# Attention and MLP kernel on one Trainium2 core: the last chunk of batch 0 in a new order, and v of block 2 transposed on TensorE

## The chip, the cores and the metric

The kernel runs on one core of a Trainium2 chip. The metric is the device time of one execution in microseconds; the time before is 698.05 us, the median of 4 runs (697.73 to 698.29). Inside one core the engines run beside each other, each working off its own queue in order: TensorE (PE) multiplies, VectorE (DVE) and ScalarE (ACT) work element by element, GpSimd (POOL) and SyncE (SP) here mainly issue DMAs. An instruction waits at the head of its queue until the semaphores it needs are set.

## What is computed

```python
# q, k, v: (4, 6080, 256) float32; w_in: (256, 2048); w_out: (2048, 256)
qn = q / (np.linalg.norm(q, axis=1, keepdims=True) + 1e-06)
kn = k / (np.linalg.norm(k, axis=1, keepdims=True) + 1e-06)
s = kn.transpose(0, 2, 1) @ qn / tau          # (4, 256, 256)
a = softmax(s, axis=-1)
x = (v @ a).reshape(4 * 6080, 256)
h = x @ w_in
out = gelu_tanh(h) @ w_out                    # (24320, 256)
```

The norms run over the 6080 tokens, so all of a batch's q and k must have been read before its 256x256 attention matrix exists. The kernel folds that matrix into the first weight: h = v @ (a @ w_in), with `aw` = a @ w_in, so that per token only two large products are left.

## The kernel before

**Statistics of a batch.** q^T k (the Gram matrix G) and the sums of squares are collected over chunks of rows. For batch 0 this stands ahead of everything else (lines 846 to 882): six chunks `c`, each loaded by GpSimd DMAs that turn float32 into bf16. For each chunk ACT squares q and DVE squares k (`square`, L192 and L194), DVE adds the halves of the squares (L211), TensorE adds the column sums (`ss_rows`: `SS[0]` for q at L268, `SS[1]` for k at L274) and the Gram rows (`gram_row`, L247; two matmuls of 256 columns a row). `warm(n)` (L369) issues n matmuls on zeros whose result nobody reads. The last chunk comes in five pieces (`PIECES`: q rows 0 to 3, k rows 0 to 4, k rows 5 to 7, q rows 4 and 5, q rows 6 and 7), squared piece by piece by `square_rows` (L202 on ACT, L204 on DVE). Its steps stand one by one at lines 863 to 882, with a `warm(6)` at L866 ahead of them.

**From the statistics to the first product.** Line 891 issues `warm(8)`; `pe_vt(0)` (L324) transposes v of block 0 on TensorE with eight 128x128 transposes into PSUM, and `pe_vt_copy` (L330) copies them to SBUF on DVE in two halves. `scores` turns G and the sums into exp(s): on ACT `lnk` (L294), `rk` (L296), `lnq` (L298) and `rq` (L300), on DVE G times rk (L304), on ACT the exponential `eT` (L306). `first_aw` multiplies eT with the first 512 columns of w_in (`sums` L350, `aw_ps` L345), takes a reciprocal (L353) and scales on DVE (L363) and ACT (L361).

**Blocks.** The 24320 tokens are worked in 48 blocks of 512 tokens (12 a batch, the last one 448). Block n has steps: `g0` to `g7` are quarter-products h = aw^T v^T of 2x512 columns into one of two PSUM pairs ("h" or "b", L520; four matmuls of 512 columns each), `G0` to `G7` their gelu on ACT (L530). From block 2 on some of these pairs are replaced by `w0...` and `w1...` sets, a seven-product scheme (Strassen's) on halves of the block: products at L596, sums of weights `SW` (L547 to L550), sums of v `vs` (L558 to L561), with ACT copies `cq` and `y5`, DVE additions `ap` and `ax`, and gelus `Gq`, `Gr`, `Gx`. The second product uses the same scheme on all blocks: `T1a` to `T4b` are its sums on DVE (L686, L698 to L702), `M1A` to `M7B` its products (L725; four matmuls of 256 columns each), then `cq`, `y5` (L735), `ap` (L775), `ax`, `c11a` (L741) and the 32x32 transposes `c..` (L750) into the tile that is stored. `pA11` to `pS4` prepare the w_out weights in block 0 and 1 (L657 to L675), and `aw2` to `aw7` with `ac2` to `ac7` make the rest of `aw` in block 0 (L460, L473).

**What sets the order.** Nothing is scheduled at run time: `ORDER` (L976) holds one string of steps for each of 41 kinds of block, `WINDOW` (L971) says which string a block takes, and the loop at L965 issues the steps in that order on all engines. `+1` or `-1` behind a step makes it one of the next or the last block. Statistics of the next batch (`row`, `qsq`, `f1` and so on) are mixed into the blocks.

**How v comes in.** Blocks 0 and 1 load v straight into an SBUF tile (`load_v0`, L314) and transpose it on TensorE (`pe_vt`, in block 1's case by the steps `vtp`, `vtc0` and `vtc1` in block 0's string). All others are cast to bf16 in DRAM by a GpSimd DMA (`cast_v`, L152, step `lv`) and read back by a transposing DMA on SP's queue (`load_vt`, L162, step `lt`). Block 2's cast is at L890, its transposing load the step `lt+2` in block 0's string. The tile of `load_v0` has the tag "ot" (three buffers), shared with the folded squares `a1_..`, the two w_out temporaries `wf0` and `wf1`, and the output tiles; the PSUM tile of `vtp` has the tag "s", shared with `aw4`, `aw6` and the `RB` accumulators of block 2 on.

Of the kernel before, what the change touches and what calls it, by code (L numbers as in the profile page):

```python
# [18 lines left out]
def kernel(  # L19
# [800 lines left out]
    with tc.manual_schedule():  # L820
# [24 lines left out]
        WARM = [0, 4, 8, 8, 10, 6]  # L845
# [17 lines left out]
        c = nch - 1  # L863
        ss_rows(c - 1, 1)
        ss_rows(c - 1, 0)
        warm(WARM[c])  # L866
        square_rows(c, 0, 0, 4, "act")
        ss_rows(c, 0, range(0, 4))
        square_rows(c, 1, 0, 5, "dve")
        for i in range(4):  # L870
            gram_row(0, c, i)
        ss_rows(c, 1, range(0, 5))
        square_rows(c, 1, 5, 8, "dve")
        square_rows(c, 0, 4, 6, "dve")
        for i in (4, 5):
            gram_row(0, c, i)
        ss_rows(c, 1, range(5, 8))
# [10 lines left out]
        load_v0(1)  # L888
        load_wout(1)
        cast_v(2)  # L890
# [24 lines left out]
        def step(what, n):  # L915
# [20 lines left out]
            elif what in ("qsq", "ksq"):  # L936
                square(b, c, "qk".index(what[0]), "act")
            elif what == "f1":
                fold(b, c)
            elif what in ("f2", "f3", "f4"):  # L940
                fold_more(b, c, int(what[1]))
            elif what == "vtp":
                pe_vt(1, "s")
            elif what[:3] == "vtc":
                pe_vt_copy(1, int(what[3]))
            elif what[0] == "p":
                prep_wout(what)
            elif what == "lt":
                load_vt(n)
            elif what == "lv":  # L950
                cast_v(n, GATE[0])
            elif what in ("lq", "lk"):
                load_one(b, c, "qk".index(what[1]), GATE[0])
            else:
                mm2_step(n, what)
# [17 lines left out]
    24, 25, 26, 15, 16, 17, 18, 19, 20, 27, 28, 29, 30, 31, 32, 33, 34, 35, 36, 36, 37,  # L973
    38, 39, 40,
]
ORDER = [  # L976
    """g0 lt+2 lv+3 aw3 G0 aw2 ac3 g1 ac2 aw5 G1 aw4 lq+1 ac5 g2 SW0 g3 G2 ac4 aw7 G3 aw6 ac7 g4
    ac6 g5 T1a G4 lk+1 vtp G5 g6 vtc0 pA11 g7 G6 vtc1 T2a M1A G7""",
    """g0 pF0-1 lt+2 lv+3 M1B-1 G0 g1 pS1-1 pF1-1 G1 M5A-1 M5B-1 cq-1 g2 pS2-1 lq+1 T2b-1 g3 G2
    pS4-1 M6A-1 G3 M6B-1 g4 pS3-1 y5-1 g5 G4 ap-1 T1a M3A-1 G5 w0m1+1 M3B-1 lk+1 T3b-1 g6  # L980
    pA12-1 vs+1 g7 G6 c12-1 T3a-1 M7B-1 G7 M2B-1 T4a-1 M2A-1 T4b-1 pNA-1 M7A-1 w0m5+1 ax-1""",
    """g0 w0cq T3b-1 lt+2 w0y5 lv+3 row1-1 c11a-2 M4A-2 G0 T2b-1 w0m6 M5B-1 w0ap row3-1 ksq-1
    M4B-2 T2a-1 w0m2 w0m7 row0-1 w0ax w0m3 g3 w0Gq c21-2 lq+1 T3a-1 M5A-1 G3 M1B-1 T4a-1 M1A-1
    c22-2 w0Gx g4 SW1-2 y5-1 cq-1 g5 c11-2 G4 lt+3 lv+4 vs+1 w0m4 M6B-1 w0Gr M6A-1 qsq-1 g6
    ap-1 T1a lk+1 M3A-1 G6 row2-1 M3B-1 f1-1 w0m1+1 G5 M7A-1 T4b-1 w0m5+1 M7B-1 w0y5+1 c12-1
    row5-1 row3 ax-1 w0cq+1 row2 T2a row4-1 g7 ksq f2-1 w0m6+1 row0 w0ap+1 M4B-1 G7 M2A-1
    M2B-1 qsq M4A-1 c11a-1""",
    """g0 f3-2 c21-2 w0m7 G0 w0m2 T2b-1 w0m3 M5A-1 w0ax M1A-1 w0Gq T3a-1 g3 vs+1 w0Gx M1B-1 G3
    w0m4 f1-1 lq+1 M5B-1 g4 cq-1 c22-2 w0Gr w1m5 T1a G4 M6B-1 M6A-1 lt+3 lv+4 w1m1 y5-1 row1-1
    f2-1 w1cq g7 ap-1 w1y5 T4b-1 w1m6 G7 row5-1 w1ap M3A-1 lk+1 row4-1 T3b-1 M3B-1 qsq w0m5+1  # L990
    c12-1 w1m7 w1m2 w1ax w1m3 M7B-1 w1Gq T4a-1 M2A-1 w1m4 c11-2 M2B-1 w1Gr T2a M7A-1 w0y5+1
    row0 ax-1 w0m1+1 w1Gx""",
    """g0 c11a-2 w0cq T3b-1 M4A-2 G0 T3a-1 row5-1 w0m6 M4B-2 f3-2 ksq-1 row2-1 w0ap g3 c21-2
    T2b-1 w0m3 G3 w0m7 w0m2 w0ax M5B-1 lq+1 M1A-1 w0Gq T4a-1 M1B-1 f4-2 w0m4 cq-1 M5A-1 w0Gr
    f1-1 w1m5 M6A-1 y5-1 w1m1 M6B-1 f2-1 w1cq lt+3 lv+4 g4 ap-1 w1y5 c22-2 w0Gx w1m6 c11-2
    M3B-1 w1ap G4 M7B-1 vs+1 row3-1 M3A-1 qsq lk+1 w1m7 f3-1 g7 w1ax T4b-1 w1m3 G7 row4-1 w1m2
    c12-1 w1m4 row1-1 f4-1 M7A-1 w1Gr row2 w1Gq ax-1 M2A-1 T1a w0m1+1 w0m5+1 M2B-1 w0y5+1""",
    """g0 T2a-1 w0cq w1Gx-1 M4A-2 c11a-2 T4a-1 w0m6 G0 M4B-2 w0ap M5A-1 ksq-1 M5B-1 c22-2 c21-2
    row1-1 w0m2 vs+1 w0m7 w0m3 g3 w0Gq w0ax lq+1 T2b-1 M1B-1 G3 w0m4 c11-2 M1A-1 T3a-1 g4 w0Gr
    f1-1 cq-1 w1m5 G4 row4-1 M6A-1 lt+3 lv+4 T4b-1 w1m1 M6B-1 f2-1 y5-1 w1cq g7 ap-1 w1y5  # L1000
    T3b-1 w1m6 G7 M3A-1 w1ap lk+1 M3B-1 M7B-1 w0Gx c12-1 w1m7 ksq M7A-1 w1ax w1m3 w0m5+1 ax-1
    w1m2 w1m4 T1a M2A-1 w1Gr M2B-1 w1Gq row4 c11a-1 row3-1 w0m1+1 f3-1 row0-1 w0cq+1 M4B-1
    c11-1 M4A-1 w0y5+1 row5-1 qsq c21-1 w0m6+1""",
    """g0 w0ap f4-2 M5A-1 w1Gx-1 w0m3 c22-2 w0m7 G0 w0m2 w0ax row2-1 M1A-1 w0Gq T3a-1 M1B-1 w0m4
    T2a-1 g3 cq-1 T3b-1 w0Gr lq+1 M5B-1 G3 f1-1 g4 T2b-1 row0-1 G4 w1m1 M6A-1 T4a-1 w1m5 f2-1
    M6B-1 lt+3 lv+4 y5-1 w1cq g7 ap-1 w1y5 f3-1 w1m6 w0Gx row1-1 w1ap M3B-1 G7 M3A-1 vs+1 lk+1
    w1m7 w1m2 ksq row5-1 w1ax M7B-1 M7A-1 c12-1 T1a w1m3 w1m4 M2A-1 w1Gr M2B-1 ax-1 w1Gq
    w0m5+1 T4b-1 row3-1 w0m1+1 row1 c11a-1 w0cq+1 row0""",
    """g0 T2a-1 w0y5 c11-2 w1Gx-1 w0m6 M4B-2 w0ap G0 M4A-2 f4-2 row4-1 w0m3 qsq-1 w0m7 c22-2 g3
    w0ax w0m2 c21-2 G3 M5A-1 T2b-1 lq+1 w0m4 M1A-1 f1-1 w0Gr row3-1 M1B-1 w0Gq T4a-1 row5-1  # L1010
    w1m1 w1m5 T4b-1 cq-1 M5B-1 w1cq g4 f2-1 lt+3 lv+4 w1y5 T3a-1 w1m6 y5-1 M6A-1 G4 w1ap
    row2-1 M6B-1 f3-1 w0Gx w1m2 T3b-1 w1m3 w1m7 qsq lk+1 g7 ap-1 w1ax M7A-1 f4-1 G7 M3B-1 vs+1
    w1m4 M3A-1 w1Gr M7B-1 c12-1 w1Gq row1 ax-1 w0m5+1 w0m1+1 T1a M2A-1 w0cq+1 M2B-1 w1Gx""",
    """g0 c22-2 w0y5 c11a-2 row2-1 T3a-1 G0 w0m6 M4B-2 w0ap M5B-1 ksq-1 T2b-1 M4A-2 w0m7 c21-2 g3
    w0ax M1A-1 f1-1 G3 w0m2 w0m4 M1B-1 T2a-1 w0Gr w0m3 M5A-1 f2-1 cq-1 T3b-1 row4-1 w0Gq w1m5
    w1m1 c11-2 M6B-1 T4b-1 y5-1 M6A-1 w0Gx lt+3 lv+4 g4 ap-1 w1cq T4a-1 w1y5 M3A-1 f3-1 G4
    w1m6 M3B-1 w1ap row3-1 M7A-1 qsq c12-1 w1m3 vs+1 M7B-1 g7 ax-1 ksq T1a row4 row0 w1m7
    M4A-1 w1ax M2A-1 G7 f4-1 M2B-1 w1m4 c11a-1 row5-1 w1Gr w1m2 f1 M4B-1 w1Gq row1 row2 row0-1
    f2 row5 w0m5+1 f3 w0m1+1 T3a""",
    """lq+4 g0 w0cq c21-2 w0y5 M5B-1 T2a-1 G0 w0m6 M1A-1 w0ap M1B-1 w1Gx-1 f4-1 row3-1 w0m7 cq-1  # L1020
    g3 T2b-1 gc w0ax w0m3 G3 w0m2 M5A-1 T4a-1 w0m4 ss c11-2 w0Gr T3b-1 w0Gq w1m5 sv M6A-1
    T4b-1 pow w1m1 y5-1 M6B-1 c22-2 w1cq g4 lt+3 lv+4 ap-1 w1y5 vs+1 w1m6 G4 M7A-1 w1ap lk+4
    M7B-1 kf M3A-1 w0Gx ax-1 g7 kr T1a w1m7 G7 M3B-1 w1m3 c12-1 w1m2 krp w1ax w1Gq M4A-1 S1+1
    w0m5+1 w1m4 S0+1 w1Gx M2A-1 T2a w1Gr M2B-1 T3a w0y5+1 M4B-1 w0m1+1 th0+1 c21-1""",
    """g0 w0cq c22-2 c11a-2 th1 M1B-1 T3b-1 G0 M1A-1 T2b-1 w0m6 M5A-1 dn w0ap g3 cq-1 rc0 w0m7 G3
    w0m3 w0m2 w0ax M6B-1 lq+4 M5B-1 rc1 w0Gq w1m5 w0m4 M6A-1 rc2 w0Gr g4 y5-1 lt+3 lv+4 w1y5
    ap-1 w1m1 rc3 M3B-1 w1cq M3A-1 G4 vs+1 w1m6 M7B-1 w1ap w0Gx g7 c12-1 eT w1m7 G7 M2A-1 w1ax
    w1m3 w1m2 M7A-1 T4b-1 w1Gq M2B-1 T4a-1 lk+4 w1m4 rsum+1 ax-1 w0m5+1 w1Gr""",
    """g0 rs T1a-1 w0y5 w0m1 aw0 w0cq M4B-2 ac0 G0 M4A-2 c11-3 w0m6 aw1 w1Gx-1 w0ap g3 ac1 c21-2
    T2b-1 w0m7 w0m3 G3 aw2 w0ax M1B-1 c11a-2 w0Gx w0m2 ac2 w0m4 M1A-1 w0Gr T3b-1 M5B-1 w0Gq  # L1030
    w1m5 T2a-1 aw3 w1m1 cq-1 M5A-1 ac3 lt+3 lv+4 w1cq g4 vs+1 y5-1 w1y5 aw4 SW0 G4 M6B-1 w1m6
    M6A-1 ac4 w1ap g7 lq+4 ap-1 T3a-1 w1m7 aw5 c22-2 w1m2 w1m3 ac5 w1ax M7B-1 G7 T1a M3B-1
    M3A-1 w1Gx w1m4 w0m5+1 c12-1 w1Gr M7A-1 c11-2 aw6 w1Gq T4b-1 w0m1+1 M2B-1 ax-1 w0y5+1
    T4a-1 M2A-1 w0cq+1""",
    """g0 T2b-1 ac6-1 c11a-2 w0m6 G0 M4A-2 w0ap M4B-2 c22-2 aw7-1 c21-2 w0m7 g3 ac7-1 w0ax M1A-1
    G3 M1B-1 SW1-1 lk+3 w0m4 w0m2 cq-1 w0m3 T3b-1 M5A-1 w0Gr T2a-1 M6B-1 w0Gq M5B-1 vs+1 w1m1
    w1m5 y5-1 M6A-1 T3a-1 lt+3 lv+4 w1cq g4 ap-1 w1y5 T4a-1 w0Gx w1m6 M3B-1 w1ap G4 M7A-1
    M3A-1 c11-2 w1m2 c12-1 w1m3 w1m7 w1Gq g7 w1ax M7B-1 G7 w1m4 ax-1 M2A-1 T4b-1 M2B-1 w1Gr
    M4A-1 T1a w1Gx M4B-1 w0m5+1 w0m1+1 w0y5+1""",
    """g0 lq+3 c21-2 T3a-1 w0cq M1A-1 c11a-2 G0 T2a-1 w0m6 M1B-1 c22-2 M5A-1 ksq w0ap g3 T3b-1  # L1040
    w0m7 cq-1 row2 w0ax G3 row1 M5B-1 T2b-1 row3 w0m4 y5-1 w0m2 T4a-1 w0Gr w0m3 M6A-1 w0Gq
    c11-2 w1m5 w1m1 lt+3 lv+4 row4 M6B-1 w1cq g4 ap-1 w1y5 lk+3 T4b-1 w0Gx w1m6 M3A-1 G4 w1ap
# [179 lines left out]
```

## Time and profile before

| what | value |
|---|---|
| median of 4 runs | 698.05 us (697.73 to 698.29) |
| the profiled execution | 697.99 us, of which the span from first to last instruction is 696.2 us |
| granted TensorE clock, mean | 0.997 |
| instructions in the span | 14406 |
| first matmul of block 0 (`g0`, L520) | starts 38.23 us after the span's start |
| eight transposes of block 1 (L324) | 46.01 us, the next matmul starts at 46.46 us |
| v of block 2: the SP queue's first transposing loads (L162) | issued from 48.23 us on |

The profile's page gives busy times by engine, the span in 40 slices, the chain of work that ended last, and the costliest groups of instructions. The timeline lists one engine's instructions in order of time, runs of equal ones merged into one row: start, duration, what it is, how many, and in brackets how long the engine stood idle before and who ended the wait. A matmul's duration overlaps that of the next one, so the time that a run of matmuls takes from TensorE is read from its start to the start of the next row.

### The profile page before, as it was taken

How to read it: one execution, taken by the hardware profiler on the slowest of the kernel's cores; microseconds unless marked ns; L12 is line 12 of the kernel's file. 1: busy time of each engine (PE TensorE's matmuls, PEld its weight loads, DVE VectorE, ACT ScalarE, POOL GpSimd, SP SyncE). 2: the span in 40 equal slices, each digit the busy share in tenths (PEclk: the TensorE clock that was granted, in tenths of full speed). 3: DMA queues.
4: the chain of work that ended last, by engine and by line, in shares of the span. 5: the costliest groups of instructions: out<-in, count | busy, mean ns of one | idle time of the engine just before them, and what ended most of it. 6: DMA issues, size and time to landing. Idle time of an engine off the chain costs nothing.

```text
span 696.2 us, 14406 instructions
## 1 busy us (share of the span) xinstructions
PE 675.1 (97%) x5499; PEld 530.4 (76%) x5499; DVE 629.9 (90%) x1243; ACT 616.5 (89%) x894; POOL 72.9 (10%) x135
## 2 busy tenths in 40 slices
PE   3899999999999999999999999999999999999996
PEld 2756777777777777777777777777777888888785
DVE  4489899999998889999999889999999999999996
ACT  5289999998889999998888999999888999999993
POOL 4321100111001001101010010010000000000000
PEclk9999999999999999999999999999999999999998
DMA  9999987786777987647687777683573464453315
GB/s 243 207 262 138 139 153 121 124 106 98 120 131 113 132 127 114 109 81 126 87 136 121 118 125 125 96 137 56 79 106 63 77 103 76 70 98 59 59 34 88
DMA packets 161733, 79.33 MB, mean 114 GB/s; under 512 B 149472, under 2 KB 152672, under 8 KB 160672
## 3 DMA queue, kind: packets, MB, share of 16 engines
q0 software_dynamic: 13952, 39.72, 35.5%
q1 hardware_dynamic: 146608, 37.41, 32.8%
q10 hardware_dynamic: 1104, 1.28, 0.5%
q8 instruction: 43, 0.70, 0.4%
q14 instruction: 26, 0.21, 0.1%
HBM read 78.91 MB, written 36.83 MB: 166 GB/s over the span
## 4 chain that ended last, share of the span: by engine, by line
PE 93%; DMA 4%; DVE 1%; issue 0%; ACT 0%; POOL 0%; DVEq 0%; ACTq 0%; POOLq 0%
PE r L725 23%; PE h L520 22%; PE p L725 17%; PE rb L596 13%; PE qp L596 9%; PE G L247 5%; DMA t<-in_k_dram 2%; PE awp L460 2%; DMA t<-in_q_dram 1%; PE ss L281 0%; DVE xw L620 0%; PE ss L274 0%; PE warm L369 0%; PE rk L405 0%; DVE t L686 0%
## 5 line engine op out<-in xcount | busy, mean ns | idle before, releaser
L725 PEld LDWEIGHTS <-wcomb 128*128 128x128 bf16 x2688 | 262.3, 98 | 42.8 <-issue 0.2
L530 ACT ACTIVATE g<-h 128x1024 bf16<-128x1024 f32 (+1 forms) x178 | 179.6, 1013 | 16.3 <-PE h L520 14.9
L725 PE MATMUL r<-t,wcomb 128*128 128x256 bf16 (+1 forms) x1152 | 164.7, 271 | 0.1
L520 PE MATMUL h<-vT,aw 128*128 128x512 bf16 (+1 forms) x648 | 164.6, 377 | 0.1
L622 ACT ACTIVATE g<-qp 128x1024 bf16<-128x1024 f32 (+1 forms) x103 | 104.6, 1015 | 5.8 <-PE qp L596 3.9
L725 PE MATMUL p<-g,wcomb 128*128 128x256 bf16 (+1 forms) x760 | 106.7, 272 | 0.0
L520 PEld LDWEIGHTS <-aw 128*128 128x128 bf16 x712 | 69.4, 98 | 49.0 <-issue 0.7
L596 PEld LDWEIGHTS <-sw 128*128 128x128 bf16 x824 | 80.2, 98 | 27.5 <-issue 0.9
L192 ACT ACTIVATE sq<-t 128x1536 bf16<-128x1536 bf16 (+4 forms) x59 | 79.3, 1359 | 7.3 <-DMA t<-in_q_dram 7.3
L617 DVE TENSOR_TENSOR qp<-rb,yw 128x512 f32<-128x512 f32 (+1 forms) x103 | 70.9, 689 | 12.8 <-PE rb L596 8.8
L596 PE MATMUL rb<-tv,sw 128*128 128x256 bf16 (+1 forms) x412 | 78.0, 271 | 0.2 <-DVE qp L617 0.2
L620 DVE TENSOR_TENSOR xw<-rb,yw 128x512 f32<-128x512 f32 (+1 forms) x103 | 69.5, 674 | 4.9 <-PE rb L596 4.1
L596 PEld LDWEIGHTS <-aw 128*128 128x128 bf16 x618 | 60.4, 98 | 13.0 <-issue 1.4
L612 ACT ACTIVATE qp<-rb 128x512 f32<-128x512 f32 (+1 forms) x103 | 59.7, 580 | 10.4 <-PE rb L596 5.8
L630 ACT ACTIVATE g<-xw 128x512 bf16<-128x512 f32 (+1 forms) x103 | 63.3, 625 | 1.5 <-DVE xw L620 1.5
L615 ACT ACTIVATE yw<-qp 128x512 f32<-128x512 f32 (+1 forms) x103 | 61.2, 594 | 4.0 <-PE qp L596 2.1
L627 ACT ACTIVATE g<-rb 128x512 bf16<-128x512 f32 (+1 forms) x103 | 61.2, 596 | 3.8 <-PE rb L596 2.6
L698 DVE TENSOR_TENSOR t<-g,t 128x1024 bf16<-128x1024 bf16 (+1 forms) x96 | 63.6, 666 | 0.6
L700 DVE TENSOR_TENSOR t<-g 128x1024 bf16<-128x1024 bf16 (+1 forms) x96 | 63.8, 671 | 0.0
L702 DVE TENSOR_TENSOR t<-t,g 128x1024 bf16<-128x1024 bf16 (+1 forms) x96 | 63.4, 668 | 0.0
L247 PE MATMUL G<-t 128*128 128x256 bf16 (+1 forms) x352 | 58.1, 273 | 1.4 <-DMA t<-in_k_dram 1.4
L686 DVE TENSOR_TENSOR t<-g 128x2048 bf16<-128x2048 bf16 (+1 forms) x48 | 57.4, 1195 | 0.1
(131 smaller groups left out, 878.7 us busy)
## 6 DMA issues: line engine op xcount, KB each, us to landing
out_dram<-ot SPq DMA_DIRECT2D x174, 128.0 KB, 3.1
vb<-in_v_dram POOLq DMA_DIRECT2D x42, 256.0 KB, 4.6
t<-in_q_dram POOLq DMA_DIRECT2D x21, 384.0 KB, 5.2
t<-in_k_dram POOLq DMA_DIRECT2D x21, 384.0 KB, 6.7
wst<-in_moe_w_out_dram POOLq DMA_DIRECT2D x2, 1024.0 KB, 10.4
t<-in_q_dram POOLq DMA_DIRECT2D x3, 512.0 KB, 15.1
t<-in_k_dram POOLq DMA_DIRECT2D x3, 512.0 KB, 17.0
out_dram<-ot SPq DMA_DIRECT2D x12, 112.0 KB, 2.5
```

Source lines behind the costliest of these rows:

```text
L192: nc.scalar.activation(o, t[:np_, r, :], AF.Square)
L247: nc.tensor.matmul(G[b][:, jc, :], lhsT=qt[:np_, r, jc * 128 : jc * 128 + 128], rhs=kt[:np_, r, :], start=first and jc == 0, stop=jc == 1, ...
L520: mm = nc.tensor.matmul(hp[:, u, :cols], lhsT=AW[b][:, cc, fc * 128 : fc * 128 + 128], rhs=vt_tiles[n][:, cc, :cols], start=cc == 0, stop= ...
L530: nc.scalar.activation(gs(n)[:, 2 * p : 2 * p + 2, :cols], HP.pop((n, p))[:, :, :cols], AF.Gelu_apprx_tanh)
L596: GATE[0] = nc.tensor.matmul(acc[:, u * hc : u * hc + hc], lhsT=lhs[:, u * 128 : u * 128 + 128], rhs=rhs, start=m in (1, 5) and u == 0, st ...
L617: nc.vector.tensor_add(qp(n, i)[:, 1, :c], RB[n, i][:, :c], YW[n, i][:, :c])
L620: nc.vector.tensor_add(XW[n, i][:, :c], RB[n, i][:, :c], YW.pop((n, i))[:, :c])
L622: nc.scalar.activation(gs(n)[:, 2 * pa : 2 * pa + 2, :c].rearrange("p u (t x) -> p t u x", t=2), QP.pop((n, i))[:, :, :c].rearrange("p t ( ...
L698: nc.vector.tensor_sub(o, quarter(n, 1, 1, f0, f1), ts[1][:, f0:f1, :hc])
L700: nc.vector.tensor_sub(o, quarter(n, 1, 1, f0, f1), quarter(n, 0, 1, f0, f1))
L702: nc.vector.tensor_sub(o, ts[2][:, f0:f1, :hc], quarter(n, 1, 0, f0, f1))
L725: nc.tensor.matmul(ACCS[n, acc][:, :hc], lhsT=wcomb[:, w, fc, :], rhs=x, start=first and k == 0, stop=k == 3, skip_group_check=True)
```

## The change

In the last chunk of batch 0 the `warm(6)` goes, and the steps move: the Gram rows 0 to 3 stand ahead of the q sums of rows 0 to 3, and the k sums of rows 5 to 7 ahead of the Gram rows 4 and 5. Nothing on ACT or DVE moves there.

Block 2's `cast_v(2)` and `lt+2` go. `load_v0(2)` loads its v into an SBUF tile, in GpSimd's queue behind block 1's v and ahead of the second half of w_out; the new steps `vtq`, `vtr0` and `vtr1` transpose it on TensorE (eight transposes, PSUM tag "s") and copy it on DVE (two copies).

Blocks 0 to 16 have new strings in `ORDER`. They hold the same steps but for those named; steps move between neighbouring blocks. Most of block 2's `w0` set now stands in block 1's string, and `T2a`, `M1A` move from block 0's string into block 1's. From block 17 on, every block keeps its steps; in blocks 18, 21, 25 and 30 a few neighbouring ones are exchanged.

```diff
-        WARM = [0, 4, 8, 8, 10, 6]
+        WARM = [0, 4, 8, 8, 10]
...
         ss_rows(c - 1, 1)
         ss_rows(c - 1, 0)
-        warm(WARM[c])
         square_rows(c, 0, 0, 4, "act")
-        ss_rows(c, 0, range(0, 4))
         square_rows(c, 1, 0, 5, "dve")
         for i in range(4):
             gram_row(0, c, i)
+        ss_rows(c, 0, range(0, 4))
         ss_rows(c, 1, range(0, 5))
         square_rows(c, 1, 5, 8, "dve")
         square_rows(c, 0, 4, 6, "dve")
+        ss_rows(c, 1, range(5, 8))
         for i in (4, 5):
             gram_row(0, c, i)
-        ss_rows(c, 1, range(5, 8))
         ss_rows(c, 0, range(4, 6))
         square_rows(c, 0, 6, 8, "dve")
...
         load_v0(1)
+        load_v0(2)
         load_wout(1)
-        cast_v(2)
         warm(8)
...
+            elif what == "vtq":
+                pe_vt(2, "s")
+            elif what[:3] == "vtr":
+                pe_vt_copy(2, int(what[3]))
...
-    """g0 lt+2 lv+3 aw3 G0 aw2 ac3 g1 ac2 aw5 G1 aw4 lq+1 ac5 g2 SW0 g3 G2 ac4 aw7 G3 aw6 ac7 g4
-    ac6 g5 T1a G4 lk+1 vtp G5 g6 vtc0 pA11 g7 G6 vtc1 T2a M1A G7""",
-    """g0 pF0-1 lt+2 lv+3 M1B-1 G0 g1 pS1-1 pF1-1 G1 M5A-1 M5B-1 cq-1 g2 pS2-1 lq+1 T2b-1 g3 G2
-    pS4-1 M6A-1 G3 M6B-1 g4 pS3-1 y5-1 g5 G4 ap-1 T1a M3A-1 G5 w0m1+1 M3B-1 lk+1 T3b-1 g6
-    pA12-1 vs+1 g7 G6 c12-1 T3a-1 M7B-1 G7 M2B-1 T4a-1 M2A-1 T4b-1 pNA-1 M7A-1 w0m5+1 ax-1""",
...
+    """g0 lv+3 aw3 G0 aw2 g1 ac2 ac3 aw4 G1 aw5 lq+1 ac4 g2 ac5 g3 G2 aw6 G3 g4 ac6 SW0 aw7 G4 g5
+    lk+1 ac7 vtp G5 pA11 g6 vtc0 g7 vtc1 G6 T1a vtq G7""",
+    """g0 vtr0-1 vtr1-1 lt+2 lv+3 g1 T2a-1 G0 T2b-1 M1B-1 G1 pF0-1 g2 g3 G2 pS1-1 w0m1+1 pF1-1
+    lq+1 M1A-1 G3 g4 cq-1 pS2-1 pNA-1 g5 pS4-1 M6B-1 G5 M5A-1 pS3-1 M6A-1 G4 M5B-1 g7 vs+1
+    y5-1 g6 ap-1 G7 T3a-1 lk+1 M3A-1 T3b-1 pA12-1 M7A-1 T4b-1 w0m5+1 M7B-1 w0cq+1 row0 ax-1
+    row1 w0y5+1 M3B-1 T4a-1 G6 w0m6+1 M4B-1 c12-1 w0ap+1 M4A-1 qsq M2A-1 c21-1 M2B-1 row2
+    c11a-1 M1B ksq T1a w0m2+1 w0m7+1 w0m3+1""",
...
```

## Prediction, on record before the changed kernel's time was known

> **What bounds the kernel now.** I read the page's busy shares and chain first, then TensorE's timeline and waits, stretch by stretch. The page:
>
> ```profile
> PE 675.1 (97%) x5499; PEld 530.4 (76%) x5499; DVE 629.9 (90%) x1243; ACT 616.5 (89%) x894; POOL 72.9 (10%) x135
> ...
> PE 93%; DMA 4%; DVE 1%; issue 0%; ACT 0%; POOL 0%; DVEq 0%; ACTq 0%; POOLq 0%
> ```
>
> TensorE is busy 97% of the span and 93% of the chain that ends last; the 4% of DMA are the loads of batch 0's q and k. The table by stages (length, then busy time of PE, PEld, DVE, ACT, POOL, then the clock) says where TensorE is free at all:
>
> ```profile
> 38.30:140.00 101.70, 101.70 (x764) 74.35 (x765) 93.24 (x177) 94.97 (x122) 13.31 (x25) 1.00 0.90 155
> 140.00:200.00 60.00, 59.77 (x474) 45.75 (x472) 57.51 (x117) 53.38 (x82) 7.26 (x12) 1.00 0.72 108
> 200.00:300.00 100.00, 100.00 (x807) 78.53 (x805) 90.64 (x181) 94.51 (x131) 10.48 (x20) 1.00 0.84 123
> ```
>
> From 38.30 us on it is never idle but for 0.23 us between 140 and 200. Since ends of matmuls are modelled, I checked it start to start: four products of 512 columns take 39.10 - 38.23 = 0.87 us, two aw parts (39.10 to 39.97) 0.87 us, eight products of 256 columns (50.80 to 51.67) 0.87 us, and this pace holds. So from there on the time is the sum of TensorE's instructions plus few waits, and a change gains only by a shorter start, fewer instructions or fewer waits. The start, on TensorE:
>
> ```profile
> 28.48 1.91 PE L247 MATMUL G<-t 128*128 128x256 bf16 x16 [1.12 <-DMA t<-in_k_dram]
> 30.23 1.04 PE L274 MATMUL ss<-sq,ones_bf 128*128 128x256 bf16 x8
> 31.10 0.54 PE L268 MATMUL ss<-ones_bf,sq 128*128 128x1 bf16 x16
> 31.50 0.81 PE L369 MATMUL warm<-zeros_bf,ones_bf 128*128 128x256 bf16 x6
> 32.16 0.34 PE L268 MATMUL ss<-ones_bf,sq 128*128 128x1 bf16 x8
> 32.36 1.03 PE L247 MATMUL G<-last,last 128*128 128x256 bf16 x8
> 33.23 0.71 PE L274 MATMUL ss<-sq,ones_bf 128*128 128x256 bf16 x5
> 33.77 0.60 PE L247 MATMUL G<-last,last 128*128 128x256 bf16 x4
> 34.21 0.49 PE L274 MATMUL ss<-sq,ones_bf 128*128 128x256 bf16 x3
> 34.54 0.24 PE L268 MATMUL ss<-ones_bf,sq 128*128 128x1 bf16 x4
> 34.64 0.60 PE L247 MATMUL G<-last,last 128*128 128x256 bf16 x4
> 35.08 0.24 PE L268 MATMUL ss<-ones_bf,sq 128*128 128x1 bf16 x4
> 35.18 1.03 PE L369 MATMUL warm<-zeros_bf,ones_bf 128*128 128x256 bf16 x8
> 36.05 0.61 PE L324 MATMUL vt_ps<-ident_bf,v 128*128 128x128 bf16 x8
> ```
>
> After the k load that lands at 28.44 no row has a bracket: TensorE's own queue, the warm-ups included, is the bound up to 36.5, not the loads.
>
> **Part 1, the last chunk.** The `warm(6)` takes 32.16 - 31.50 = 0.65 us. Without it everything behind moves up by that, if its data are there:
> - Gram rows 0 to 3 now start at 31.50. They need q rows 0 to 3 (issued 14.22, 15.4 to land: 29.6) and k rows 0 to 4 (14.75 + 16.5 = 31.25): there, with 0.25 to spare. They end at 32.37, the q sums (0.20) at 32.58.
> - k sums of rows 0 to 4: DVE squared them from 31.30 to 32.13; there. To 33.12. Those of rows 5 to 7: squared by 32.80; there. To 33.45. Before, these ended at 34.54: 1.09 us earlier.
> - Gram rows 4 and 5 to 33.89; q sums to 33.99; Gram rows 6 and 7 need the last piece (20.61 + 12.9 = 33.5): there. To 34.42, q sums (squares of DVE end 33.92) to 34.53. Before 35.18: 0.65 earlier.
> - `warm(8)` and the eight transposes of block 0 (v: 23.37 + 11.4 = 34.8, needed at 35.4) end at 35.85 instead of 36.50.
>
> ACT's chain moves up more. Its lnk waited for the k sums; now lnk, rk run from 33.65 to 34.57, lnq waits for the q sums at 34.7, rq ends at 35.27, and eT's first half lies between 35.33 and 35.85 instead of 36.21 and 36.72. So the `sums` start at 35.9, not 36.77 (0.87 earlier), but DVE's two copies of vt start only 0.65 earlier (36.05) and hold the reciprocal and the scaling that the first `g0` waits for (38.23, 0.18 idle, released by DVE). `g0` starts 0.65 to 0.75 earlier; I take **-0.70**, 37.53. The w_in pieces (26.55 + 9.0 = 35.6 for the first, the second 28.73 + 7.5 = 36.2) are needed at 35.97 and 36.58: there, by 0.3 to 0.4 us only. GpSimd's queue is the same up to block 1's v. Bounds: 0, if one of these landings is late by that much; -0.87, if DVE's copies follow eT.
>
> **Part 2, v of block 2.** Added on TensorE are eight transposes. The trace has them: they start at 46.01 in block 0, the next matmul at 46.46: **+0.45**, on a queue that is never idle, so in full. Added on DVE are two copies, 0.42 long each and 0.34 apart, 0.68 in all. DVE is busy 11.65 of 12.15 us between 48.63 and 60.78, so whether that is free must be counted. In the new strings TensorE's queue behind `g0` is eight g (6.93), six aw (2.60) and two sets of transposes (0.90): block 1 starts at 47.96, and its `M3A-1` comes after eight g, six M (2.61) and one small product (0.22), at 57.7, `M7A-1` at 58.15. DVE's queue from the two copies at 48.14: copies 0.67, T2a and T2b 1.20, pF0 1.25, pS1 0.61, pF1 1.25, pS2 0.61, pS4 1.14, pS3 1.13, vs 0.99 (starts of the same operations between 47.93 and 58.18): `ap`, which M3A needs, ends at 57.4, T3a, which M7A needs, at 58.0. Both in time, by 0.3 and 0.15 us. What makes room is T1a of block 1 (1.13 us), which stood at 55.46 ahead of this and now comes behind it. So: 0.
>
> Moved on queues: in GpSimd's queue block 2's load takes the place behind block 1's v and pushes the second half of w_out (issued 35.87, 1 MB) behind it in the DMA engines, which are full there (about 200 GB/s). It costs 1.1 us by the distance of the landings of block 1's v (34.34 + 9.8 = 44.1) and of the w_out half ahead of it (33.44 + 9.6 = 43.0), at most 2.6 us (512 KB at 200 GB/s). The second half landed at 35.87 + 11.3 = 47.2, so now at 48.3 to 49.8; pF0 needs it at 50.0: covered. Block 2's v itself lands at about 45.3, needed at 47.5. SP's queue loses one transposing load (48.23), so block 3's stands first in it; block 2's was not late before (first use 57.19), so nothing is gained by that.
>
> [...]
>
> **Part 3, the new order of blocks 1 to 16.** The products are the same, so their sum is. What can change are waits. TensorE's of before in this stretch, start to start: 158.41 (0.34 late after eight products from 157.20), 173.48 (0.10 late), 183.79 (0.23 late), some 0.8 with smaller ones, all in 140 to 200, where DVE is busy 57.51 of 60. Best case: they all go, -0.8. Worst: three more like the longest, +1.0. The new strings have the same products between a result and its next use in DVE's loops (0.87 us at least, as before), so the row nearest to it is the old stretch itself: **0**.
>
> Sum: 697.99 - 0.70 + 0.45 + 0 = 697.74, say 697.7. The profiled execution lies 0.06 under the median of 698.05, less than the runs differ, and I add nothing for it.
>
> **Rivals.**
> - *The waits go too* (696.9 = 697.74 - 0.8). For: block 2's products come earlier and the stretch up to batch 1's end is freshly ordered. Against: DVE is as full there as before, and the other batches have such waits in the same place.
> - *DVE becomes the bound in block 1* (slower): the two copies delay T2a to T3a, and M3A, M7A wait. Place: 57 to 59 us. Price: up to the copies, 0.68: 698.4. It decides from 0.15 us on by which DVE is later than my count. For: 11.65 of 12.15 busy. Against: T1a's 1.13 us moved behind.
> - *The head gives nothing* (the part does not do what it says): w_in's or the last q piece's landing takes the warm-ups' place as the bound, and the transposes are paid all the same: 697.99 + 0.45 = 698.4. For: 0.3 us of cover. Against: every landing of before lies ahead of its need.
> - *New waits in blocks 3 to 16*, 1.5 us and more (699.5): for it speaks only that nothing in the old profile can show these strings.
>
> **How the numbers follow.** Forecast 0.57; waits go 0.16; DVE 0.11; head 0.09; new waits 0.07. The forecast's own range is 697.3 to 698.1; to hold 8 in 10 with the rivals it goes from 696.8 to 698.7. About 0.2% (1.4 us) is what a measurement of this kernel can tell from no change. Faster by more needs all waits gone and more: 0.06. Slower by more is the last rival: 0.08. Within: 0.86.
>
> **What would show it.** `g0` at 37.5 and no `warm` at 31.5; k sums done by 33.6; eight transposes 0.45 us start to start just ahead of block 1's g0 at 48.0; no bracket on TensorE from 38 to 62; M3A of block 0 near 57.7. Wrong would be a bracket there that names DVE or a DMA, a clock under 1.00, or idle time of TensorE above 1 us between 60 and 270.

## The result and the profile after

| | time, us | ratio to the kernel before |
|---|---|---|
| before | 697.98 (697.72 to 698.97, 58 runs) | |
| after | 696.9 (696.68 to 697.27, 40 runs) | 0.9985, 95% interval 0.998 to 0.9989 |
| forecast | 697.7, range 696.8 to 698.7 | |

The change takes 1.1 us off, within the 0.2% that the forecast called "within" and 0.8 us below its number. The profiled execution of after took 696.86 us with a span of 695.1, against 697.99 and 696.2: 1.13 us to account for. The page of after, busy shares and chain:

```profile
PE 675.0 (97%) x5501; PEld 530.2 (76%) x5501; DVE 630.3 (91%) x1245; ACT 616.1 (89%) x894; POOL 73.0 (11%) x135
...
PE 95%; DMA 4%; DVE 0%; issue 0%; POOL 0%; ACT 0%; DVEq 0%; POOLq 0%
```

TensorE is the bound as before. The table by stages from `g0` on (length, then busy time of PE, PEld, DVE, ACT, POOL, then the clock) shows that the 0.23 us of idle time between 140 and 200 have all but gone. That holds for busy time, with its modelled ends; start to start most of TensorE's waits there are still present (the list of places below):

```profile
37.40:140.00 102.60, 102.60 (x776) 75.10 (x777) 94.31 (x181) 94.48 (x121) 13.74 (x26) 1.00 0.88 151
140.00:200.00 60.00, 59.99 (x474) 45.68 (x472) 56.98 (x116) 54.62 (x84) 6.58 (x12) 1.00 0.73 112
```

The start on TensorE, some rows of the timeline of after:

```profile
28.36 1.91 PE L247 MATMUL G<-t 128*128 128x256 bf16 x16 [1.23 <-DMA t<-in_k_dram]
...
31.38 1.03 PE L247 MATMUL G<-last,last 128*128 128x256 bf16 x8
...
32.45 1.03 PE L274 MATMUL ss<-sq,ones_bf 128*128 128x256 bf16 x8
33.32 0.60 PE L247 MATMUL G<-last,last 128*128 128x256 bf16 x4
...
35.27 0.61 PE L324 MATMUL vt_ps<-ident_bf,v 128*128 128x128 bf16 x8
...
37.40 1.04 PE L520 MATMUL h<-vT_pe,aw 128*128 128x512 bf16 x4 [0.36 <-DVE aw L363]
```

No `warm` stands at 31.5, the k sums end before the Gram rows at 33.32, and `g0` starts at 37.40 instead of 38.23. From the Gram rows that wait for the k load to `g0` it is 37.40 - 28.36 = 9.04 us, against 38.23 - 28.48 = 9.75 before: 0.71 less. The rest of the 0.83 is that the load came earlier. The bracket says what is late next: DVE, whose reciprocal and scaling stand behind its two copies of vt (the transposed v of block 0). Block 1 on TensorE, after:

```profile
47.36 0.61 PE L324 MATMUL vt_ps<-ident_bf,v 128*128 128x128 bf16 x8
47.80 1.90 PE L520 MATMUL h<-vT_pe,aw 128*128 128x512 bf16 x8
...
57.57 0.60 PE L725 MATMUL p<-g,wcomb 128*128 128x256 bf16 x4
58.01 0.60 PE L725 MATMUL r<-t,wcomb 128*128 128x256 bf16 x4
```

The eight transposes take 47.80 - 47.36 = 0.44 us, `M3A` (57.57) and `M7A` (58.01) run without a bracket.

I laid the start times of the same TensorE products side by side in both traces. Where the distance between them changes, it is won or lost:

| place | after against before, us | what it is |
|---|---|---|
| `g0` | -0.83 | the head; 0.12 of it because the k load landed at 28.32 instead of 28.44 |
| block 1 | +0.45 | eight transposes |
| 60 to 257 us | -0.11 | waits of 0.9 in all before, 0.8 after, at other places |
| 331 to 337 us | -0.37 | two waits of before are shorter or gone |
| 364 us | +0.12 | a new wait for ACT |
| 593 us | -0.24 | a wait of before is gone |
| behind the last matmul | -0.14 | last stores |
| sum | -1.12 | |

The first three lines sum to -0.49, or -0.37 without the earlier k load, near the forecast's -0.25. The rest comes from blocks in which the change altered no step, or only the place of a load. That was the open question, beside whether the parts are worth what the sum gave them.

### The profile page after: what moved, and what is told of

Its sections match the earlier page's. It is cut to its first block, busy times and chain, and to the rows that moved or that the text cites. A ratio compares the mean times of both kernels' runs of the same rounds, so it can differ in the third digit from the quotient of the medians.

```text
span 695.1 us, 14411 instructions
## 1 busy us (share of the span) xinstructions
PE 675.0 (97%) x5501; PEld 530.2 (76%) x5501; DVE 630.3 (91%) x1245; ACT 616.1 (89%) x894; POOL 73.0 (11%) x135
## 4 chain that ended last, share of the span: by engine, by line
PE 95%; DMA 4%; DVE 0%; issue 0%; POOL 0%; ACT 0%; DVEq 0%; POOLq 0%
PE r L725 24%; PE h L520 22%; PE p L725 18%; PE rb L596 13%; PE qp L596 10%; PE G L247 5%; DMA t<-in_k_dram 2%; PE awp L460 2%; DMA t<-in_q_dram 1%; PE ss L281 0%; PE ss L274 0%; PE vt_ps L324 0%; PE rk L405 0%; PE warm L369 0%; DVE vT_pe L330 0%
## 5 line engine op out<-in xcount | busy, mean ns | idle before, releaser
L520 PE MATMUL h<-vT,aw 128*128 128x512 bf16 (+1 forms) x624 | 158.5, 377 | 0.0
```

Of the source, the lines that this page charges most:

```text
L520: mm = nc.tensor.matmul(hp[:, u, :cols], lhsT=AW[b][:, cc, fc * 128 : fc * 128 + 128], rhs=vt_tiles[n][:, cc, :cols], start=cc == 0, stop= ...
```

## The experiments

Theory A of e1 to e4 was the prediction's sum, in which the parts are independent: the head -0.70, the transposes +0.45, the order 0. The ratio of each run is to runs of the kernel before on the same chip and beside it (697.88 us for e1 to e4, 697.92 for e13, 697.90 for the others).

| run | what | us | ratio, 95% interval |
|---|---|---|---|
| e1_head | before, new last chunk alone | 698.77 | 1.0014, 1.0004 to 1.0023 |
| e2_nowarm | before without `warm(6)`, old order of its steps | 698.38 | 1.001, 0.9999 to 1.0021 |
| e3_oldhead | after with the old last chunk | 697.65 | 0.9996, 0.9988 to 1.0005 |
| e4_vt2 | before, block 2's v on TensorE, old strings | 699.31 | 1.0021, 1.0013 to 1.003 |
| c_after | the changed kernel again | 697.08 | 0.9986, 0.9978 to 0.9995 |
| e8_both | before, both parts, old strings | 698.73 | 1.0011, 1.0002 to 1.002 |
| e5_dma2 | after, block 2's v by DMA | 704.65 | 1.01, 1.0085 to 1.0116 |
| e9_late | after, swaps in blocks 18 to 30 taken back | 697.08 | 0.9985, 0.9977 to 0.9994 |
| e11_after7 | after, 7 idle memsets on DVE | 698.11 | 1.0004, 0.9995 to 1.0012 |
| e12_before6 | before, 6 idle memsets on DVE | 697.29 | 0.9991, 0.9982 to 1.0 |
| e6_nowarm8 | after without `warm(8)` | 696.65 | 0.9982, 0.9974 to 0.9991 |
| e13_sum | e6, one copy moved to ACT, ACT's numbers moved by 3 | 696.76 | 0.9983, 0.9974 to 0.9993 |

### The head alone: e1, e2 and e3

e1 is the first part of the diff alone. e2 keeps the old order of the last chunk's steps:

```diff
-        warm(WARM[c])
```

> The kernel of before with the new last chunk alone (no warm(6), steps in the new order); blocks and block 2's v as before. Theory A, the head carries what the changed kernel's trace shows (g0 at 37.4 instead of 38.2): 0.7 to 0.8 us less, about 697.2, with the waits of TensorE at 158, 173, 183, 331 and 593 us where they were, only earlier. Rival B, most of the gain is the new order of the blocks: 0.3 us less or under, 697.7. Rival C, the waits at 331 and 593 us, which sit in strings that nothing changed, belong to the execution or to the place of the code and not to the edit: then some of them are gone or others come here too, 697.2 less or more 0.4.

> The kernel of before with only the warm(6) taken out; the steps of the last chunk stay in their old order. Theory A, TensorE's queue is the bound up to the transposes of block 0: everything behind moves by the 0.65 us that the six take, 697.35, g0 at 37.6. The new order of the steps would then be worth the rest to e1, 0.05 to 0.2 us. Rival, a late piece of q or k takes the place: 697.7 to 698.0 and a bracket with a DMA on TensorE between 31.5 and 35.

Theory A failed in both by the median: `g0` started 0.69 and 0.90 us earlier (0.25 of the 0.90 by an earlier k load), and the time rose in e1 and did not fall in e2, whose interval holds 1. TensorE's timelines of before, e1 and e2 say where it went:

```profile
56.44 0.38 PE L596 MATMUL rb<-vT,aw 128*128 128x256 bf16 x2
```

```profile
55.31 0.60 PE L725 MATMUL p<-g,wcomb 128*128 128x256 bf16 x4
56.59 0.38 PE L596 MATMUL rb<-vT,aw 128*128 128x256 bf16 x2 [0.69 <-DMA vT<-vb]
```

```profile
56.85 0.38 PE L596 MATMUL rb<-vT,aw 128*128 128x256 bf16 x2 [1.14 <-DMA vT<-vb]
```

`w0m1`, the first product on block 2's v, waits for the transposing load. Start to start it is 0.85 us late (1.31 in e2). In before it started at 56.44 without a wait. The landing did not only fail to move up with the start: it came later. The load is issued when block 2's cast has landed, and that cast, issued 0.48 us earlier in e1 (36.27 instead of 36.75), took 12.1 instead of 11.5 us. Issued at 48.1 to 48.4, the load landed 6.1 us later in before (54.3), 8.2 later in e1 (56.6), 8.7 in e2 (56.8). What else moved is GpSimd's queue: its cast of a later block's v waits for a product of TensorE, and is issued at 49.26 in e1 instead of 49.95. Between 51 and 58 us the largest burst of that queue's packets (229 KB in one microsecond, at 54) lies in e1 ahead of SP's (247 KB at 56); in before SP's (234 KB at 53) came first. That the one pushed the other back is inferred; the packets do not say which transfer they belong to, and no run isolates it.

The profiled execution of e1 took 698.14 us, the second shortest of 11 (698.06 to 699.47); -0.69 and +0.85 explain it, but not the 0.6 us more of the median. e2's executions reach from 697.46, near theory A, to 702.26, where the kernel before beside them stays within 697.62 to 698.27. So the landing seems to vary from one execution to the next; each run has one trace, so this is not shown.

e3 is the other half: after, but with the last chunk of before.

> The changed kernel with the old last chunk (warm(6) back, old order of its steps). Theory A: the changed kernel's 696.9 plus 0.7 to 0.8, so 697.7, that is 0.3 less than before although eight transposes are added. Rival B, the new order is what gains: 697.2. Rival C, the rest beside the head is chance of where waits fall: anything from 697.7 to 698.4 (before plus 0.45).

It took 697.65, 0.6 to 0.8 more than after: in the changed kernel the head is worth the 0.70 of the sum. From the k load's Gram rows to `g0` e3 takes 9.75 us, as before does.

### Block 2's v alone, and both parts in the old strings: e4 and e8

e4 has the second part of the diff, with `vtq` at the end of block 0's old string and the copies at the head of block 1's:

```diff
+        load_v0(2)
         load_wout(1)
-        cast_v(2)
...
-    ac6 g5 T1a G4 lk+1 vtp G5 g6 vtc0 pA11 g7 G6 vtc1 T2a M1A G7""",
-    """g0 pF0-1 lt+2 lv+3 M1B-1 G0 ...
+    ac6 g5 T1a G4 lk+1 vtp G5 g6 vtc0 pA11 g7 G6 vtc1 T2a M1A vtq G7""",
+    """g0 vtr0-1 vtr1-1 pF0-1 lt+2 lv+3 M1B-1 G0 ...
```

e8 adds the new last chunk to it.

> The kernel of before with block 2's v loaded straight and transposed on TensorE, in the old strings: vtq behind M1A in block 0's string, vtr0 and vtr1 at the start of block 1's. Theory A, the eight transposes cost what they take on a full TensorE and the two copies are hidden: 0.45 more, 698.4. Rival D, DVE becomes the bound in block 1 as the copies stand ahead of pF0: up to 0.68 more than that, 699.1, with a bracket that names DVE between 48 and 62. Rival E, the transposing load was in somebody's way: 698.0.

> The kernel before with parts 1 and 2 but without part 3: the new last chunk and block 2's v on TensorE, in the old strings (the eight transposes at the end of block 0's string, the two copies at the head of block 1's). Theory A, the parts add as the prediction summed them: 0.70 less and 0.45 more, 697.6. Theory B, each part alone meets a wait and only one of the two goes when they are put together: block 2's v is no longer late at 56 us, but DVE's copies still stand ahead of the preparation of w_out and TensorE waits 0.7 us for wcomb near 50 us: 697.9 - 0.7 + 0.45 + 0.7 = 698.4. Theory C, that wait is set by the landing of the second half of w_out, a fixed time: the earlier start makes it 1.4 us and nothing of the head is kept: 699.1.

e4's 699.31 is near rival D's 699.1. e8 is theory B, 0.3 us over its 698.4: in its trace the k load came 0.2 us later than in before, and its late waits (0.28 at 438, 0.30 at 590 us) stand in place of those of before at 173, 331 and 593. TensorE's timeline of e8 has the wait:

```profile
49.88 1.03 PE L520 MATMUL h<-vT_pe,aw 128*128 128x512 bf16 x4
51.45 1.05 PE L725 MATMUL p<-t,wcomb 128*128 128x256 bf16 x8 [0.55 <-DVE wcomb L662]
```

`M5A` of block 0 waits for `wcomb`, 0.71 us start to start in e4 and e8 alike: DVE prepares w_out behind the two added copies. So the rival "DVE becomes the bound in block 1" is real. The new strings avoid it: in after `M5A` stands four g steps later. Part 3 was priced at 0, but without it the two other parts cost 698.73 - 697.08 = 1.65 us more. Of these 0.71 are this wait, 0.58 the two late ones and 0.2 the k load.

### Block 2's v by DMA in the new strings: e5

```diff
-        load_v0(2)
         load_wout(1)
+        cast_v(2)
...
-    """g0 lv+3 aw3 ...    lk+1 ac7 vtp G5 pA11 g6 vtc0 g7 vtc1 G6 T1a vtq G7""",
-    """g0 vtr0-1 vtr1-1 lt+2 lv+3 g1 ...
+    """g0 lt+2 lv+3 aw3 ...    lk+1 ac7 vtp G5 pA11 g6 vtc0 g7 vtc1 G6 T1a G7""",
+    """g0 lt+2 lv+3 g1 ...
```

> The changed kernel with its new strings, but block 2's v cast to DRAM and loaded by the transposing load as before; the eight transposes and DVE's two copies are gone. Theory A, block 2's v by DMA is in time (as the prediction held): 0.45 us less than the changed kernel, 696.4. Theory B, its landing is what the earlier start and the earlier first use run into: it landed near 57.2 us in the run with the new last chunk alone, and the new strings use it first at 51.7 - 0.45 = 51.3: a wait of 5 to 6 us on TensorE, released by SP's queue, and 701 to 702.

Theory B, and more than it said. TensorE's timeline of e5:

```profile
57.28 0.58 PE L596 MATMUL rb<-vT,aw 128*128 128x256 bf16 x2 [5.24 <-DMA vT<-vb]
57.66 1.06 PE L725 MATMUL r<-g,wcomb 128*128 128x256 bf16 x4
58.51 2.83 PE L520 MATMUL h<-vT_pe,aw 128*128 128x512 bf16 x8
```

The transposing load lands at 57.2 and TensorE waits 5.24 us. Then four products of 256 columns take 58.51 - 57.66 = 0.85 us, twice the 0.44 that they take in after (57.57 to 58.01). The same trace by stages gives the reason in the clock's column:

```profile
57.20:60.20 3.00, 2.92 (x10) 1.43 (x10) 1.01 (x3) 1.33 (x2) 0.55 (x1) 0.50 0.79 144
```

The clock granted after the pause is 0.50. Start to start, the pause costs 5.4 and the slow stretch 1.5 us. With two more waits (0.5 for a gelu at 47 us, 0.4 more than in after at 178) and without the 0.44 of the transposes this is 7.4 of the 7.6 us by which e5 is over c_after.

### The late gains: c_after, e9, e11, e12

c_after is the changed kernel again, e9 has the four swaps of steps in blocks 18 to 30 undone (for instance `g0 lq+3` back to `lq+3 g0`).

> The changed kernel once more, beside the three kernels of this call that are made from it. All theories: 696.9 us, ratio 0.9985 to the kernel before. If the late differences (no wait on TensorE at 331 and at 593 us, where the kernel before has 0.29 and 0.22 us) belong to the program, they are absent here too; if they are chance of one execution, one of them is back.

> The changed kernel with the four swaps of neighbouring steps in the strings of blocks 18, 21, 25 and 30 taken back (loads before or after g0, before or after a row step). Theory A, the late gains (0.29 us at 331, 0.22 at 593, minus 0.12 at 364) come from these swaps: the waits are back and it takes 697.3. Theory B, they follow from everything that stands before (phase of the engines after the changed part): 696.9 as the changed kernel, with the same waits as it.

c_after has after's waits at the same products, each within 0.01 us: they belong to the program, not to one execution. e9 has them too, so the swaps are not the cause. DVE's timeline around 330 us is where before loses time, and both kernels have the same steps there. Before:

```profile
329.72 0.65 DVE L698 TENSOR_TENSOR t<-g,t 128x1024 bf16<-128x1024 bf16 x1
330.87 0.69 DVE L620 TENSOR_TENSOR xw<-rb,yw 128x512 f32<-128x512 f32 x1 [0.50 <-PE rb L596]
```

After:

```profile
329.23 0.65 DVE L698 TENSOR_TENSOR t<-g,t 128x1024 bf16<-128x1024 bf16 x1
330.00 0.69 DVE L620 TENSOR_TENSOR xw<-rb,yw 128x512 f32<-128x512 f32 x1
```

From `t` to `xw` it is 1.15 us before and 0.77 after. The bracket names TensorE's rb, but in before DVE's wait on its semaphore ended at 330.45 and `xw` started 0.41 later. TensorE's timeline of before shows the price:

```profile
330.45 1.04 PE L725 MATMUL r<-g,wcomb 128*128 128x256 bf16 x8
331.61 0.38 PE L596 MATMUL rb<-tv,aw 128*128 128x256 bf16 x2
```

Eight products of 256 columns take 0.87 in the same trace from 50.80 to 51.67; here the next starts after 1.16. I then numbered DVE's records in the trace, waits on semaphores included, from 0. This `xw` is number 703 in before. In e4 and e8, whose DVE queue is 3 longer, it is not number 703, and it is not delayed; delays of 0.40 us stand there at numbers 959 and 1343 instead. All of them, with 319 and 1343 in before, are 63 above a multiple of 128, and each stands right behind a wait on a semaphore. Over all traces of this case, 1233 records of DVE stand right behind a wait that ended with DVE idle. The 12 of them whose number is 63 above a multiple of 128 all started 0.395 to 0.414 us after the wait's end; none of the other 1221 started more than 0.15 us after the last semaphore that it needed. After's DVE queue is 7 records shorter than before's, so other instructions have these numbers. e11 and e12 test that and change nothing else:

```diff
         nc.vector.memset(log_it, math.log(inv_tau))
+        idle = const.tile([128, 7], FP32)
+        for i in range(7):
+            nc.vector.memset(idle[:, i : i + 1], 0.0)
```

(e12 does it with 6, in the kernel before.)

> The changed kernel with seven memsets of one column each on DVE in its first two microseconds, where DVE waits for the first load; nothing reads them. They only move the number that each later instruction has in DVE's queue by 7, to what it is in the kernel before. Theory A: DVE stalls by 0.40 us at certain numbers of its queue (63 above a multiple of 128 in the traces so far: 319, 703, 959, 1343), and this delays TensorE where the instruction with that number stands right behind a semaphore wait. Then number 703 is xw of 330 us and number 1343 the product p of 590 us again, as in the kernel before: TensorE's waits of 0.29 and 0.22 us near 331 and 592 us are back, and the time is 696.9 + 0.5 = 697.4. Theory B, the late gains come from something else: 696.9 and no wait there.

> The kernel before with six such memsets on DVE. Theory A (the stall by number): numbers 319, 703, 959 and 1343 now fall on instructions that do not stand right behind a semaphore wait, only 1471 does (xw of 641.8 us): the waits at 331 and 593 us are gone without any part of the change, 0.5 less, 697.4; at most 0.2 of it comes back at 642. Theory B: 697.9 and the waits stay.

Theory A in both. DVE in e11, then in e12:

```profile
329.68 0.65 DVE L698 TENSOR_TENSOR t<-g,t 128x1024 bf16<-128x1024 bf16 x1
330.81 0.69 DVE L620 TENSOR_TENSOR xw<-rb,yw 128x512 f32<-128x512 f32 x1 [0.48 <-PE rb L596]
```

```profile
329.69 0.65 DVE L698 TENSOR_TENSOR t<-g,t 128x1024 bf16<-128x1024 bf16 x1
330.47 0.69 DVE L620 TENSOR_TENSOR xw<-rb,yw 128x512 f32<-128x512 f32 x1
```

1.13 us with the memsets in the changed kernel, 0.78 with them in the kernel before. In e11 TensorE's waits at 331 (0.28) and 593 us (0.22) are back. Two more that the expectation had not listed come from numbers 191 and 319, each the product `p` behind a wait, at 110 and 167 us: 0.25 at 110, and the wait at 171 grows from 0.15 to 0.50. So seven memsets that nobody reads cost the changed kernel 1.0 us, and it is then no faster than the kernel before (1.0004). In e12 the waits at 173, 331 and 593 are gone, and six memsets win 0.6 us; the stall feared at 642 is not there, as number 1471 falls on the wait itself and not on the instruction behind it.

### A shorter head: e6 and e13

e6 removes `warm(8)` from the changed kernel.

> The changed kernel without the last warm-up, the eight products of 256 columns ahead of block 0's transposes (TensorE is then idle for some of that time). Theory A, the head is bound by the chain eT, sums, reciprocal, aw, in which DVE's reciprocal stands behind its two copies of vt: the transposes start when v lands, near 34.8, the copies follow the scaling of S at 35.35 and the reciprocal comes 0.2 to 0.25 us earlier: g0 at 37.15 to 37.2 and 696.65. Theory B, the warm-up keeps TensorE's granted clock: it falls below 1.00 after the pause, and the time is 697 or more.

Theory A: 696.65, `g0` at 37.00, and a granted clock of 1.00 through the head. TensorE's timeline of e6:

```profile
28.12 1.91 PE L247 MATMUL G<-t 128*128 128x256 bf16 x16 [1.15 <-DMA t<-in_k_dram]
...
35.53 0.20 PE L350 MATMUL sums<-ones_bf,eT 128*128 128x1 bf16 x2 [0.42 <-ACT eT L306]
...
37.00 1.04 PE L520 MATMUL h<-vT_pe,aw 128*128 128x512 bf16 x4 [0.19 <-DVE aw L363]
```

From the k load's Gram rows to `g0` it is 8.88 us instead of 9.04: the warm-up is worth 0.16, and 0.24 of the 0.40 by which `g0` is earlier than in after is the k load. The median, 0.25 to 0.43 us under the two of the changed kernel (696.9 and 697.08, not taken beside it), fits that only in part. e13 adds two things to it:

```diff
+        idle = const.tile([128, 3], FP32)
+        nc.vector.memset(idle[:, 0:1], 0.0)
...
+        for i in range(2):
+            nc.scalar.activation(idle[:, i + 1 : i + 2], eps, AF.Copy)
...
-        warm(8)
...
-        pe_vt_copy(0, 1)
+        nc.scalar.activation(vt_tiles[0][:, 1, :], VPS[0][:, 1, :], AF.Copy)
```

> The changed kernel without the last warm-up, with the second half of block 0's vt copied on ACT instead of DVE (one memset of a column on DVE in the first microseconds keeps the numbers of DVE's queue as they were), and with two activations of one column on ACT ahead of the first load, which nothing reads: with the copy they move ACT's numbers by 3. Theory A (the stall by number holds for ACT too, where number 575 is the activation of 361 us behind whose stall TensorE waits 0.12 us at 363): no instruction right behind a semaphore wait has such a number on ACT any more, the wait at 363 is gone; and the reciprocal behind one copy instead of two brings g0 forward by up to 0.1 more. 696.65 - 0.12 - 0.1 = 696.4. Theory B, ACT's stalls are not by number: the wait at 363 stays, 696.55. Theory C, ACT's copy delays its part of aw and takes the place of the wait on DVE: 696.6 and more.

Half of it. The wait at 363 us is gone, as theory A said: ACT's activation of qp, number 575 in after, started at 361.13 behind 0.70 us of idle time. ACT in after, then in e13:

```profile
361.13 0.53 ACT L612 ACTIVATE qp<-rb 128x448 f32<-128x448 f32 x1 [0.70 <-PE rb L596]
```

```profile
360.88 0.53 ACT L612 ACTIVATE qp<-rb 128x448 f32<-128x448 f32 x1 [0.41 <-PE rb L596]
```

The moved copy gave nothing: in e6 DVE already waited 0.26 us for `sums` ahead of the reciprocal, so its copies were no longer in the way. By the median e13 is not faster than e6; its profiled execution began the head 0.44 us later, with the loads, and takes the same time from the k load's Gram rows to `g0` (8.85 us for 8.88).

## Why the forecast held and its reasons were incomplete

The signs that the prediction named for the change itself all came: `g0` near 37.5, the early k sums, 0.44 us for the eight transposes, no bracket on TensorE between its first `g0` and 62 us, `M3A` near 57.7. Its number held because the change is worth little; more than half of the 1.1 us came from elsewhere.

- **The head, -0.70.** Right: 0.71 from the k load's Gram rows to `g0`, and e3 gives 0.6 to 0.8. The bound named for it, DVE's copies ahead of the scaling, is the bracket at 37.40; e6, which frees them, makes the same stretch 0.16 shorter.
- **The transposes, +0.45.** Right: 0.44, at a granted clock of 1.00 from 47.36 to 47.80. The trace of before lists 220 ns for each, but one starts every 56 ns, and it is that pitch that the eight cost: 0.45 us in before, 0.44 in after.
- **DVE in block 1, 0.** Right for the new strings: `M3A` 57.57 and `M7A` 58.01 against 57.7 and 58.15. The rival stands 0.71 us away, and it is the new order that keeps it off (e8).
- **"block 2's was not late before (first use 57.19), so nothing is gained by that."** This step failed. 57.19 is DVE's first use; TensorE's is at 56.44. And it set a landing of before against a use of before, while the head moves the use up by 0.7 us, and the landing itself moved from 54.3 to 56.6 and later. With block 2's v by DMA the head gains nothing by the median (e1, e2), and in the new order TensorE stands still for 5.24 us (e5). Part 2 was priced as a cost of 0.45; with the new order (e8) it is the condition under which part 1 is worth anything.
- **The order, 0.** Right in the stretch that it spoke of (-0.11). The rival "The waits go too" gave 696.9, the measured time, but not by its mechanism: it placed the gain at 140 to 200 us.
- **"From 38.30 us on it is never idle but for 0.23 us between 140 and 200."** Wrong behind 300 us, where the rows shown there end. The next row of that table of before has 0.13 us of idle time,

```profile
300.00:340.00 40.00, 39.87 (x319) 30.95 (x317) 38.31 (x79) 36.31 (x54) 3.67 (x6) 1.00 0.55 92
```

and start to start TensorE's waits between 300 and 690 us, those over 0.05 us, sum to 2.7. The sum had no term for a change in them.
- **What no step held.** Some 0.5 us net in the unchanged blocks, and 0.1 of the kernel before's waits near 173 us, hang on which instruction of DVE's and ACT's queues has a certain number. Without these stalls on DVE before is at 697.29 (e12), 0.2 us over c_after: about the -0.25 of the sum. So the steps sized the change itself rightly, and the rest of the 1.1 us is luck of position, which seven idle memsets take away (e11).

The 0.14 us behind the last matmul was not followed up.

## What to carry to other kernels

Before parts of a change are priced one by one, look for the transfer that the first part runs into when it succeeds: here a load that landed at 54.3 us for a first use at 56.44 had no slack left once the start moved by 0.7, because it landed later as well, at 56.6 (e1). Measure a head from the landing that starts it: that distance is 9.75 us in before and in e3, and 8.88 in e6 for 8.85 in e13, while `g0` itself came 0.42 us later in e13 with the loads (37.42 for 37.00). In this kernel, whose TensorE, DVE and ACT are 97%, 91% and 89% busy, the place of instructions in a queue alone was worth 1.0 us (e11) and 0.6 us (e12); a few idle instructions added to both programs show whether a difference of that size hangs on it. A forecast from waits seen in one program should carry that as a term of its own.

## What the hardware showed

- **A stall by queue number.** DVE pauses 0.40 us ahead of records 191, 319, 703, 959 and 1343 where these stand right behind a wait (before, e4, e8, e11), ACT 0.32 to 0.34 us ahead of 447 and 575 (after, e11); where such a number falls on an instruction that follows running work, as in e12, nothing is seen. 319 - 191 = 128, and every one is 63 above a multiple of 128. The page of after counts 28 packets of 0.22 MB in all on a queue of kind "instruction" (queue 14), all but one of them of 8 KB. They come in step with these numbers: over all traces, 145 of the 168 records of DVE with such a number and 108 of the 126 of ACT have one of them within 3 us, against 15% and 17% for the median of the 128 places in a step, and each delayed one is followed by one 0.6 to 2.8 us later. So the delays and the packets stand together in the traces; that the packets are what holds the engine, no run shows.
- **The clock after a pause.** After 5.24 us in which TensorE stood idle, the granted clock was 0.50 for about 3 us (57.2 to 60.2 in e5, 0.98 in the stretch behind); after pauses of 1.15 us at 28 and 0.42 us at 35 it was 1.00 (e6). From which length of a pause on it falls, these runs do not show.
- **A transposing load that took longer.** The same load, issued at 48.1 to 48.4 us, took 6.1 us in before and 8.2 to 9.0 in e1, e2 and e5, in which GpSimd's loads were issued up to 0.9 us earlier. That these are the cause, no run shows.
